# Converting the weights at a later due time, and loading w_out a second time with its columns on the partitions

## The chip, the cores and the metric

The kernel runs on one core of a Trainium2 chip. The metric is the time of one execution on the device in microseconds (us). TensorE (PE) does matmuls and transposes, VectorE (DVE), ScalarE (ACT) and GpSimd (POOL) work elementwise, and SyncE (SP) issues most of the DMAs. Each engine runs its own instructions in order; semaphores tie them together.

## The reference

There are 4 x 576 = 2304 tokens with 512 features, and three parts run one after the other.

1. Attention with 8 heads of 64 features. Half of the heads see the last 32 positions, the other half every 32nd position. Its output x is 2304 x 512.
2. A gated layer: `x = ((x @ w_a) * (x @ w_b)) @ w_out`, with w_a and w_b 512 x 1536 and w_out 1536 x 512.
3. A layer of 8 experts: `logits = x @ w_gate` (512 x 8). A greedy assignment in the order of all logits gives each expert 288 tokens, and each token passes `relu(x @ w1[e]) @ w2[e]` of its expert.

w_a, w_b and w_out arrive as float64, the other tensors as float32.

## The kernel before

**Numbers.** [...] A float64 piece (128 partitions x 512 numbers, 512 KB) is loaded as pairs of 32-bit words into a tile `r`, and `from_f64` (L444) turns it into float32 with two ACT passes (on the low words, and the magnitude of the high words) and four DVE passes (a shift and mask, a merge, an addition, and a compare-and-multiply that writes the float32 piece `w_f`; the first three write the scratch tile `cc`). `Load` (L464) does this for a pair of pieces: `start` issues the loads, `finish` converts, `store` writes the float32 result back to DRAM (`wab_dram`, `wo_dram`), from where later uses reload it. Each large matmul is done as three matmuls on high and low parts (`mm3`, L434): `split` makes `wh` on POOL and `wl` on DVE out of a weight tile.

**Stages.** x is built in blocks of 256 tokens. Hidden features come in 12 chunks f of 128. `gated(s)` (L833) computes `ab`, the products of one chunk with w_a and w_b for some blocks, and multiplies them into `G`. Stages 0 to 6 run over these blocks and chunks: 0: blocks 0, 1, f 0-2; 1: blocks 2, 3, f 0-2; 2: blocks 0-3, f 3-6; 3: blocks 0, 1, f 7-11; 4: blocks 2, 3, f 7-11; 5: blocks 4, 5, all f; 6: blocks 6-8, all f. Attention of batch 0 runs ahead of stage 0, batch 1 within stage 0, batch 2 within stage 4, batch 3 within stage 5. Stage 1 needs batch 1. A chunk's first use takes the freshly converted `w_f`; every later use reloads it from `wab_dram` into a tile `wab` of the pool `raws`, which has three buffers.

**The gate.** The logits don't wait for x: `gate_weights(js)` (L746) forms W = w_out @ w_gate for six groups j of 256 rows, and `logits` multiplies G by W. For each j it loads and converts w_out's rows (two loads through `raws`), stores them for the third part of the kernel, transposes the eight 128 x 128 squares on PE against the identity (tile `tp`), copies them from PSUM to `woT` with ACT, multiplies with w_gate (`pw`, eight matmuls), copies (`wT`), and does four small matmuls (`pw` again) that end in the table `Wp`. Groups 0, 1 run in stage 3, groups 2, 3 in stage 4, groups 4, 5 in stage 5.

**Order.** The program writes no engine order by hand. Each operation is recorded with a due time, and `flush` (L234) simulates the engines and gives each the ready operation that is due first; that order is then fixed. All records have line 163 in the profile, so the rows below go by tile names. `weave` (L382) sets the due times: a generator yields (cost, gap), costs of the running matmuls move the time t on, and the next step of a chain is due after its gap. Chains that a stage brings along (attention, the gate) are due at t less 2000 ns in most stages. One background chain, `convert(range(12))` (L789), converts w_a and w_b chunk by chunk at its own pace (a step each 500 ns, ten steps a chunk, 1000 ns between chunks); its steps are due at t + 4000. `convert` also issues the loads of the next chunk and the store. A chunk that isn't yet converted when a stage wants it is converted on the spot, at the stage's due time (`split_w`, L816). SP takes a DMA at most 40 us ahead of its due time, and the stores of w_a and w_b are held back until 52 us + 3 us per chunk of simulated time.

**Room.** The pool `big` has 18 buffers for `G` (kept from its first product on), `w_f`, `cc`, `woT`, `wT`, and the w_a, w_b tiles `r`. Twelve hold `G` of blocks 0-3 by stage 4, and six more hold that of blocks 4, 5 from the ninth chunk of stage 5 on.

In the first 70 us of simulated time, idle PE time is filled with throw-away matmuls (tile `warm`, L904).

Of the kernel before, what the change touches and what calls it, by code (L numbers as in the profile page):

```python
# [8 lines left out]
F32 = mybir.dt.float32  # L9
# [5 lines left out]
AF = mybir.ActivationFunctionType  # L15
# [344 lines left out]
def tile_attention_moe_moe(  # L360
# [4 lines left out]
    vs: bass.AP,  # L365
    w_ab: bass.AP,
    w_out: bass.AP,
    w_gate: bass.AP,
    w1: bass.AP,
    w2: bass.AP,  # L370
# [3 lines left out]
    nc = plan = Plan(tc)  # L374
# [4 lines left out]
    def at(t):  # L379
        plan.prio = t  # L380

    def weave(bulk, chains, spacing=0.0, lead=0.0):  # L382

        t = clock["t"]
        live = [[c, t] for c in chains]
        running = bulk is not None
        while running or live:  # L390
            nxt = min(live + back, key=lambda c: c[1]) if live + back else None
            if nxt is not None and (nxt[1] <= t or not running):
                t = max(t, nxt[1])
                at(t + 4000 if nxt in back else t - lead)
                try:
                    cost, gap = next(nxt[0])
                    t += cost
                    nxt[1] = t + (gap if nxt in back else max(gap, spacing))
                except StopIteration:
                    (back if nxt in back else live).remove(nxt)  # L400
            else:
                at(t)
                try:
                    t += next(bulk)[0]
                except StopIteration:
                    running = False
        clock["t"] = t
        at(t)

    back = []  # L410
# [11 lines left out]
    raws = ctx.enter_context(tc.tile_pool(name="raws", bufs=3))  # L422
    big = ctx.enter_context(tc.tile_pool(name="big", bufs=18))
# [77 lines left out]
    ident = consts.tile([128, 128], F32)  # L501
# [7 lines left out]
    for h in range(2):  # L509
        s = slice(64 * h, 64 * h + 64)  # L510
# [21 lines left out]
    def ps_tp(name):  # L532
        return psA.tile([128, 512], F32, name=name, tag="tp", bufs=2)
# [212 lines left out]
    def gate_weights(js):  # L746
        for j in js:
            ld = Load([w_out[256 * j + 128 * s:256 * j + 128 * s + 128].rearrange("p (u d) -> p u d", u=1)
                       for s in range(2)], wo_dram[j], raws)
            ld.start()  # L750
            yield 0, 5000
            for _ in ld.finish():
                yield 0, 300
            yield 0, 3000
            ld.store()
            r = ld.dst.rearrange("p (s d) -> p s d", s=2)
            woT = big.tile([128, 4, 256], F32, name="woT", tag="big")
            for s in range(2):
                p = ps_tp("tp")
                for kc in range(4):  # L760
                    nc.tensor.transpose(p[:, kc * 128:(kc + 1) * 128], r[:, s, kc * 128:(kc + 1) * 128], ident)
                nc.scalar.activation(woT[:, :, 128 * s:128 * s + 128], p.rearrange("p (k f) -> p k f", k=4), AF.Copy)
                yield 440, 0 if s == 0 else 1000
            pw = ps_tp("pw")
            for kc in range(4):
                nc.tensor.matmul(pw[32 * kc:32 * kc + 32, :256], wg[:, kc, :], woT[:, kc, :], start=True, stop=True)
            wT = big.tile([128, 256], F32, name="wT", tag="big")
            nc.scalar.activation(wT, pw[:, :256], AF.Copy)
            yield 500, 900
            pw = ps_tp("pw")  # L770
            for s in range(2):
                nc.tensor.matmul(pw[:, 8 * s:8 * s + 8], wT[:, 128 * s:128 * s + 128], lsel, start=True, stop=True)
            V.tensor_copy(Wp[:, 2 * j:2 * j + 2, :8], pw[:, :16].rearrange("p (s e) -> p s e", s=2))
            yield 430, 0
# [131 lines left out]
    def begun(r):  # L906
# [5 lines left out]
    plan.floor = 0.0  # L912

    weave(None, [attention(0, (0,)), later(0, attention(0, (1,))), later(6000, attention(0, (2,))),
                 later(8000, attention(0, (3,)))])
    split_w(0)
    plan.slack = SLACK
    weave(gated(0), [later(0, attention(1, (0,))), later(2000, attention(1, (1,))), later(6000, attention(1, (2,))), later(8000, attention(1, (3,)))], 0, 2000)
    weave(gated(1), [])
    weave(gated(2), [])  # L920
    weave(gated(3), [gate_weights((0, 1))], 100, 2000)
    weave(gated(4), [attention(2, (0, 2)), later(2000, attention(2, (1, 3))), gate_weights((2, 3))], 500, 2000)
    weave(gated(5), [attention(3), gate_weights((4, 5))], 0, 2000)
    plan.flush()
    apool_cm.__exit__(None, None, None)
# [401 lines left out]
    with ahead(40000):  # L1327
        for g in range(3):
            if g % 2 == 0:
                t = big.tile([128, 2, 512], F32, name="xg", tag="big")  # L1330
# [28 lines left out]
    def ps_po(d):  # L1359
        return ps_mm("po") if d == 3 else ps_acc("po")  # L1360
# [76 lines left out]
    with ahead(40000):  # L1437
        xs, q = [], []
        for kc in range(4):
            p = ps_tp("tpi")  # L1440
            for g in range(3):
                nc.tensor.transpose(p[:, 96 * g:96 * g + 96], XG[0][g][:, 128 * kc:128 * kc + 128], ident[:96, :96])
            t = cpool.tile([128, CAP], F32, name=f"oT{kc}", bufs=1)
# [3 lines left out]
        for kc in range(4):  # L1447
            p = ps_po(kc)
# [5 lines left out]
    for e in range(E):  # L1454
# [29 lines left out]
        for d in range(4):  # L1484
            t = cpool.tile([128, CAP], F32, name=f"oT{d}", bufs=1)
# [14 lines left out]
def _laid_out(q, k, v, moe_w_a, moe_w_b, moe_w_out, moe2_w_gate, moe2_w1, moe2_w2):  # L1500

    import numpy as np

    qk = np.zeros((16, 128, 2, 608), q.dtype)
    vl = np.zeros((8, 128, 2, 9, 64), v.dtype)
    vs = np.zeros((8, 128, 6, 2, 64), v.dtype)
    for n in range(16):
        b, hp = n // 4, (0, 2, 1, 3)[n % 4]
        i = 2 * b + n % 4 // 2
        for t, x in enumerate((q, k)):  # L1510
            y = x[b, 2 * hp:2 * hp + 2].transpose(0, 2, 1).reshape(128, S)
            o = 32 * t if hp < 2 else 0
            if hp >= 2:
                y = y.reshape(128, 18, 32).transpose(0, 2, 1).reshape(128, S)
            qk[n, :, t, o:o + S] = y
        y = v[b, 2 * hp:2 * hp + 2]
        if hp < 2:
            for c in range(9):
                a = max(0, 64 * c - 32)
                vl[i, 96 - (64 * c + 64 - a):96, :, c] = y[:, a:64 * c + 64].transpose(1, 0, 2)  # L1520
        else:
            y = y.reshape(2, 18, 32, 64)
            for odd in range(2):
                for r in range(3):
                    p, nr = 64 * odd + 18 * r, (4 if r == 2 else 5) if odd else 6
                    o = 18 * odd + r
                    vs[i, p:p + 18, :nr] = y[:, :, o:o + 3 * nr - 2:3].transpose(1, 2, 0, 3)
    w_ab = np.stack([w.reshape(4, 128, 12, 128) for w in (moe_w_a, moe_w_b)])
    return {
        "qk": qk.reshape(16, 128, 1216), "vl": vl.reshape(8, 128, 1152), "vs": vs.reshape(8, 128, 768),  # L1530
        "w_ab": w_ab.transpose(3, 2, 0, 1, 4).reshape(12, 128, 1024), "w_out": moe_w_out, "w_gate": moe2_w_gate,
        "w1": moe2_w1.reshape(E, 4, 128, 4, 256).transpose(0, 3, 2, 1, 4).reshape(E, 4, 128, 1024),
        "w2": moe2_w2.reshape(E, 4, 2, 128, DM).transpose(0, 1, 3, 2, 4).reshape(E, 4, 128, 1024)}

# [24 lines left out]
```

## Time and profile before

| | |
|---|---|
| median of 3 runs | 852.51 us (849.06 to 853.31) |
| the profiled execution | 849.75 us, span 848.0 us |
| PE busy | 825.1 us, 97% of the span, 6402 matmuls |
| DVE busy | 492.5 us, 58% |
| ACT busy | 311.8 us, 37% |
| POOL busy | 161.2 us, 19% |
| mean granted TensorE clock | 0.99 of 2.4 GHz |

The span runs from the first to the last instruction; the profiled execution has 1.75 us outside it. Matmuls are pipelined: a matmul's duration reaches over the start of the next ones, so what a matmul costs PE is read from the distance of starts, not from its duration. In the rows that list idle time, the words behind the arrow name what ended it.

### The profile page before, as it was taken

What the parts mean: (1) busy time and instruction counts of PE and PEld (TensorE: products, weight loads), DVE (VectorE), ACT (ScalarE), POOL (GpSimd) and SP (SyncE); (2) the same over time, 40 slices, a digit from 0 to 9 for tenths busy, and PEclk for the clock granted to TensorE, in tenths of its full rate; (3) what the DMA queues carried; (4) which work ended last, traced back from release to release, by engine and by line L of the source; (5) the groups of instructions that cost most, each with busy time, mean ns of one, the idle gap of its engine ahead of it and who ended that gap; (6) DMA issues with size and microseconds to landing.
All of it is one profiled execution on the core that took longest, in us unless ns stands there. A gap on an engine that the chain in (4) does not pass through costs nothing.

```text
span 848.0 us, 16546 instructions
## 1 busy us (share of the span) xinstructions
PE 825.1 (97%) x6402; PEld 698.8 (82%) x6402; DVE 492.5 (58%) x1448; ACT 311.8 (37%) x841; POOL 161.2 (19%) x219
## 2 busy tenths in 40 slices
PE   9898999999999999999999999999999999999995
PEld 7776888877787878888767777778799999999995
DVE  5999985357655431223477777766265655665541
ACT  6985531356455311111323232222233432443230
POOL 2101221110111130101000000000253425443311
PEclk9899999999999999999999999999999999999998
DMA  9779752145552211121232212100275655654501
GB/s 351 282 247 413 266 199 99 51 147 190 174 177 95 75 51 50 51 75 53 79 106 76 75 50 76 50 26 26 69 215 182 187 163 196 221 185 155 176 21 37
DMA packets 33487, 114.83 MB, mean 135 GB/s; under 512 B 4608, under 2 KB 4608, under 8 KB 33408
## 3 DMA queue, kind: packets, MB, share of 16 engines
q1 hardware_dynamic: 30336, 104.36, 35.9%
q0 software_dynamic: 3072, 9.41, 3.6%
q8 instruction: 50, 0.82, 0.4%
q14 instruction: 29, 0.24, 0.1%
HBM read 94.91 MB, written 18.87 MB: 134 GB/s over the span
## 4 chain that ended last, share of the span: by engine, by line
PE 82%; DVE 7%; DMA 3%; ACT 3%; issue 2%; POOL 2%; POOLq 0%; ACTq 0%; DVEq 0%; SPq 0%
PE ab L163 33%; PE px L163 18%; PE po L163 11%; PE ph L163 9%; PE pc L163 3%; DVE cc L163 2%; PE S L163 2%; PE pl L163 1%; DVE w12l L163 1%; PE O L163 1%; PE PT L163 1%; DVE t L163 1%; PE tpo L163 1%; POOL out_dram L163 1%; DVE xl L163 1%
## 5 line engine op out<-in xcount | busy, mean ns | idle before, releaser
L163 PE MATMUL ab<-xh,wh 128*128 128x512 f32 (+1 forms) x488 | 183.2, 376 | 1.1 <-DVE nm L163 0.8
L163 PE MATMUL ab<-xl,wh 128*128 128x512 f32 (+1 forms) x488 | 179.5, 368 | 1.7 <-DVE xl L163 1.7
L163 PE MATMUL ab<-xh,wl 128*128 128x512 f32 (+1 forms) x488 | 179.1, 367 | 0.6 <-DVE wl L163 0.6
L163 PEld LDWEIGHTS ab<-xh,wh 128*128 128x128 f32 x488 | 92.3, 189 | 21.2 <-issue 4.9
L163 DVE TENSOR_TENSOR G<-a_sb,ab 128x256 f32<-128x256 f32 x108 | 41.2, 415 | 117.9 <-PE ab L163 114.8
L163 PEld LDWEIGHTS ab<-xl,wh 128*128 128x128 f32 x488 | 92.5, 190 | 16.1 <-DVE xl L163 2.1
L163 PEld LDWEIGHTS ab<-xh,wl 128*128 128x128 f32 x488 | 92.5, 190 | 16.0 <-DVE wl L163 0.9
L163 DVE TENSOR_TENSOR w12l<-w,w12h 128x1024 fp32r<-128x1024 f32 x64 | 78.5, 1234 | 40.5 <-PE po L163 31.7
L163 PE MATMUL px<-woh,gh 128*128 128x512 f32 x216 | 87.2, 404 | 0.3 <-ACT gh L163 0.3
L163 PE MATMUL px<-wol,gh 128*128 128x512 f32 x216 | 87.2, 404 | 0.0
L163 ACT ACTIVATE a_sb<-ab 128x512 f32<-128x512 f32 (+1 forms) x61 | 33.3, 546 | 138.4 <-PE ab L163 119.9
L163 POOL TENSOR_SCALAR wh<-wab 128x1024 fp32r<-128x1024 f32 x32 | 35.9, 1122 | 234.5 <-PE ab L163 210.0
L163 PE MATMUL po<-hh,w12h 128*128 128x288 f32 x256 | 76.7, 300 | 0.0
L163 ACT ACTIVATE gh<-G 128x512 fp32r<-128x512 f32 x54 | 34.1, 632 | 115.8 <-PE px L163 101.5
L163 PE MATMUL ph<-xeh,w12h 128*128 128x288 f32 x256 | 75.1, 304 | 1.4 <-DVE hl L163 0.7
L163 PE MATMUL po<-hh,w12l 128*128 128x288 f32 x256 | 75.7, 296 | 0.0
L163 PE MATMUL po<-hl,w12h 128*128 128x288 f32 x256 | 75.6, 296 | 0.0
L163 PE MATMUL ph<-xel,w12h 128*128 128x288 f32 x256 | 75.2, 296 | 0.3
L163 PE MATMUL ph<-xeh,w12l 128*128 128x288 f32 x256 | 74.7, 297 | 0.0
L163 ACT ACTIVATE w12h<-w 128x1024 fp32r<-128x1024 f32 x36 | 38.2, 1060 | 60.5 <-PE po L163 42.7
L163 PEld LDWEIGHTS ph<-xel,w12h 128*128 128x128 f32 x256 | 48.7, 190 | 1.7 <-DVE xel L163 1.6
L163 PEld LDWEIGHTS ph<-xeh,w12h 128*128 128x128 f32 x256 | 47.3, 188 | 2.8 <-DVE hl L163 2.3
(369 smaller groups left out, 1539.6 us busy)
## 6 DMA issues: line engine op xcount, KB each, us to landing
w<-in_w_dram SPq DMA_DIRECT2D x64, 512.0 KB, 3.6
wab<-wab_dram SPq DMA_DIRECT2D x32, 512.0 KB, 3.3
r<-in_w_ab_dram SPq DMA_DIRECT2D x24, 512.0 KB, 8.4
qkT<-in_qk_dram SPq DMA_DIRECT2D x16, 608.0 KB, 5.9
wab_dram<-w_f SPq DMA_DIRECT2D x12, 512.0 KB, 7.8
r<-in_w_out_dram SPq DMA_DIRECT2D x12, 512.0 KB, 3.5
x_dram<-xr SPq DMA_DIRECT2D x17, 256.0 KB, 2.1
vt<-in_vl_dram SPq DMA_DIRECT2D x7, 576.0 KB, 7.2
```

The lines of the kernel that those rows point to most:

```text
L163: op.call = lambda: getattr(engine, method)(*args, **kwargs)
```

## The change

The array `w_outT` holds the same float64 numbers as `w_out`, laid out by the host so that a group's 512 columns stand on the partitions (4 x 128) and its 256 rows follow one another. `gate_weights` still loads, converts and stores w_out's rows as before, and then loads and converts the same group from `w_outT`; the converted tile takes the place of `woT`. The transposes and the ACT copies out of PSUM are gone. The gap between the end of a conversion and what follows is 1500 ns where it was 3000. In `weave`, the background chain's steps are due at t + 12000 where it was t + 4000.

```diff
@@ weave
-                at(t + 4000 if nxt in back else t - lead)
+                at(t + 12000 if nxt in back else t - lead)
@@ gate_weights
             for _ in ld.finish():
                 yield 0, 300
-            yield 0, 3000
+            yield 0, 1500
             ld.store()
-            r = ld.dst.rearrange("p (s d) -> p s d", s=2)
-            woT = big.tile([128, 4, 256], F32, name="woT", tag="big")
-            for s in range(2):
-                p = ps_tp("tp")
-                for kc in range(4):
-                    nc.tensor.transpose(p[:, kc * 128:(kc + 1) * 128], r[:, s, kc * 128:(kc + 1) * 128], ident)
-                nc.scalar.activation(woT[:, :, 128 * s:128 * s + 128], p.rearrange("p (k f) -> p k f", k=4), AF.Copy)
-                yield 440, 0 if s == 0 else 1000
+            lt = Load([w_outT[j][:, 512 * t:512 * t + 512].rearrange("p (k f) -> p k f", k=2) for t in range(2)], None, raws)
+            lt.start()
+            yield 0, 5000
+            for _ in lt.finish():
+                yield 0, 300
+            yield 0, 1500
+            woT = lt.dst.rearrange("p (k f) -> p k f", k=4)
             pw = ps_tp("pw")
@@ _laid_out
+        "w_outT": moe_w_out.reshape(6, 256, 4, 128).transpose(0, 3, 2, 1).reshape(6, 128, 1024), "w_gate": moe2_w_gate,
```

## Rows read from the trace of the kernel before

**Rows 1.** Chain that ended last, 0 to 80 us: its shares by line.
```profile
by line: DVE cc L163 20.0%; DVE t L163 9.1%; issue 8.0%; DVE w_f L163 7.6%; PE warm L904 7.4%; ACT P L163 6.5%; DVE xl L163 6.3%; DVE wl L163 4.3%; PE ab L163 4.2%; DVE P L163 3.6%; PE S L163 3.5%; ACT Ps L163 3.2%; PE PT L163 2.4%; DVE Ps 
```

**Rows 2.** Windows, early: length, then busy PE, PEld, DVE, ACT, POOL; clock, DMA.
```profile
40.00:60.00 20.00, 17.93 (x221) 15.14 (x221) 20.00 (x102) 16.64 (x82) 1.61 (x4) 1.00 0.60 197
60.00:80.00 20.00, 17.22 (x193) 13.18 (x192) 19.70 (x49) 13.81 (x40) 2.82 (x5) 1.00 1.03 410
100.00:120.00 20.00, 20.00 (x90) 16.57 (x89) 19.44 (x37) 8.39 (x14) 7.50 (x2) 1.00 0.67 233
```

**Rows 3.** PE in order of time, 26 to 78 us: start, duration, operation [idle before].
```profile
26.96 0.80 PE L163 MATMUL ab<-xh,wl 128*128 128x256 f32 x2 [0.60 <-DVE wl L163]
...
77.49 0.50 PE L163 MATMUL ab<-xl,wh 128*128 128x512 f32 x1 [1.70 <-DVE xl L163]
```

**Rows 4.** Windows of 14 to 77.5 us, instructions on `cc` alone: their sum.
```profile
sum 63.50, DVE 32.84 ACT 9.91; mean DVE 8.21 ACT 2.48
```

**Rows 5.** The same windows, instructions on `w_f` alone: their sum.
```profile
sum 63.50, PE 0.00 PEld 0.00 DVE 13.13 POOL 3.37; mean PE 0.00 PEld 0.00 DVE 3.28 POOL 0.84
```

**Rows 6.** All engines in order of time: the first reload of stage 1.
```profile
69.47 1.05 POOL L163 TENSOR_SCALAR wh<-wab 128x1024 fp32r<-128x1024 f32 x1 [16.09 <-DMA wab<-wab_dram]
...
71.58 1.21 DVE L163 TENSOR_TENSOR wl<-wab,wh 128x1024 fp32r<-128x1024 f32 x1
```

**Rows 7.** Tile `tp`: duration in ns min/median/max, first and last start in us.
```profile
L163 PE MATMUL tp<-ident,w_f x48: 270/273/330, 151.5 to 259.6; 128*128 128x128 f32 x48
L163 ACT ACTIVATE woT<-tp x12: 570/592/599, 152.2 to 260.2; 128x512 f32<-128x512 f32 x12
```

**Rows 8.** PE in order of time: transposes and the next PE operation behind them.
```profile
151.54 1.03 PE L163 MATMUL tp<-ident,w_f 128*128 128x128 f32 x8
152.33 0.48 PE L163 MATMUL ab<-xh,wh 128*128 128x512 f32 x1
...
183.72 0.66 PE L163 MATMUL tp<-ident,w_f 128*128 128x128 f32 x4
184.21 0.49 PE L163 MATMUL PT<-ident,P 128*96 128x128 f32 x3
...
258.79 1.03 PE L163 MATMUL tp<-ident,w_f 128*128 128x128 f32 x8
259.76 0.88 PE L163 MATMUL S<-qkT 64*64 64x96 f32 x16
```

**Rows 9.** Tiles `r`, `cc` and `w_f`: the passes of all 36 conversions, columns as in Rows 7.
```profile
L163 ACT ACTIVATE r<-r x36: 654/677/708, 14.2 to 236.5; 128x512 int32<-128x512 uint32 x36
L163 DVE TENSOR_SCALAR cc<-r x36: 409/419/1276, 15.2 to 240.4; 128x512 int32<-128x512 int32 x36
L163 DVE SCALAR_TENSOR_TENSOR cc<-r,cc x36: 617/683/726, 15.7 to 240.8; 128x512 int32<-128x512 int32 x36
L163 DVE CUSTOM_DVE_ANT_0 cc<-r,cc x36: 671/683/1533, 16.6 to 241.6; 128x1024 uint16<-128x1024 uint16 x36
L163 DVE SCALAR_TENSOR_TENSOR w_f<-cc x36: 629/683/1271, 17.9 to 244.4; 128x512 f32<-128x512 f32 x36
```

**Rows 10.** Windows of stages 3 to 5, columns as in Rows 2.
```profile
135.00:151.50 16.50, 16.50 (x74) 13.65 (x73) 10.24 (x18) 1.79 (x3) 3.32 (x4) 1.00 0.25 96
187.30:197.30 10.00, 8.27 (x122) 6.24 (x121) 5.49 (x31) 7.52 (x33) 0.17 (x1) 0.83 0.73 250
213.00:280.00 67.00, 66.63 (x593) 53.19 (x593) 36.32 (x135) 31.92 (x117) 10.81 (x15) 1.00 0.42 135
```

**Rows 11.** SP and DVE in order of time: a gate piece, and a reloaded chunk.
```profile
176.91 0.33 SPq L163 DMA_DIRECT2D r<-in_w_out_dram  x1
...
184.46 0.69 DVE L163 CUSTOM_DVE_ANT_0 cc<-r,cc 128x1024 uint16<-128x1024 uint16 x1
...
234.83 0.33 SPq L163 DMA_DIRECT2D wab<-wab_dram  x1
...
248.69 1.22 DVE L163 TENSOR_TENSOR wl<-wab,wh 128x1024 fp32r<-128x1024 f32 x1
```

More of the change, by code (lines that the diff above doesn't have):

```diff
@@ L367, in tile_attention_moe_moe @@
     w_out: bass.AP,
+    w_outT: bass.AP,
     w_gate: bass.AP,
@@ L1530, in _laid_out @@
         "qk": qk.reshape(16, 128, 1216), "vl": vl.reshape(8, 128, 1152), "vs": vs.reshape(8, 128, 768),
-        "w_ab": w_ab.transpose(3, 2, 0, 1, 4).reshape(12, 128, 1024), "w_out": moe_w_out, "w_gate": moe2_w_gate,
+        "w_ab": w_ab.transpose(3, 2, 0, 1, 4).reshape(12, 128, 1024), "w_out": moe_w_out,
+        "w_outT": moe_w_out.reshape(6, 256, 4, 128).transpose(0, 3, 2, 1).reshape(6, 128, 1024), "w_gate": moe2_w_gate,
         "w1": moe2_w1.reshape(E, 4, 128, 4, 256).transpose(0, 3, 2, 1, 4).reshape(E, 4, 128, 1024),
```

## The prediction

> **What bounds the kernel now.** I read the windows by stage first, because the page's 97% for PE hides two regimes. From 78 us on PE has work nearly all the time; stage 5 has 66.63 of 67 us busy [rows 10]. There, PE work that goes is time that goes. Before 78 us it is otherwise: from 40 to 60 us PE is busy 17.93 of 20 us and DVE all 20, from 60 to 80 us PE 17.22 and DVE 19.70 [rows 2]. The reader is to see that DVE is the full engine and PE the one that waits, 4.85 us in these 40. The chain of waits for the first 80 us agrees: the largest single share is the conversion, 20.0% on `cc` and 7.6% on `w_f`, more than the softmax of attention, 9.1% on `t` [rows 1]. The end of this regime is a wait of PE: stage 1 has begun and stops for 1.70 us until 77.49 us for an `xl`, the last piece of attention of batch 1 [rows 3]. From there on PE runs through, so a start of stage 1 that is earlier by some time ends the kernel earlier by the same, if nothing new waits.
>
> One hole lies in the second regime. From 187.3 to 197.3 us, where stage 4's matmuls are short and attention of batch 2 ends, PE is busy 8.27 of 10 us at a granted clock of 0.83 [rows 10]. 1.73 us are idle, and the mean clock of 0.83 means that the lower level (1.2 in place of 2.4 GHz) took another 0.17 x 10 = 1.7 us, behind the thin work there.
>
> **The transposes.** 48 transposes go, in nine runs: three of 8 and six of 4. A transpose lasts 273 ns [rows 7], but eight of them start within 1.03 us. The cost on PE is the distance from the first of a run to the next other operation: 152.33 - 151.54 = 0.79 us for the first run, 184.21 - 183.72 = 0.49 for one of four, 259.76 - 258.79 = 0.97 for the last [rows 8]. The nine distances sum to 2.72 (the eights) + 2.87 (the fours) = 5.6 us. One of the fours, 0.5 us, lies in the hole, where PE waits anyway. So 5.1 us come off the end. The bounds are 0, if PE waited at each place for something else, and 48 x 0.273 = 13.1 us, if a transpose cost its duration. The distance is the nearest row to what is asked, and I take it.
>
> The Trainium skill (TensorE: Matmul & The Clock Gate, Part 4: PE-mode transpose) gives about 275 ns for a 128 x 128 transpose in one kernel's context and says that access latency is most of it. The duration in this trace agrees [rows 7]; the distances of the starts do not let it be taken as the cost. By the page's figure the saving would be 13.2 us, an estimate.
>
> Twelve ACT copies of 0.592 us go with them, 7.1 us [rows 7], on an engine that is busy 1.79 of 16.5 us there [rows 10].
>
> **The second load and conversion.** Per group two loads of 512 KB and two conversions, so 12 of each. A conversion is four DVE passes, 0.419 + 3 x 0.683 = 2.47 us by their durations, and two ACT passes of about 0.68 us [rows 9]. That is 48 passes or 29.6 us more on DVE, and 24 passes or 16.2 us more on ACT (9.1 net of the copies). What hides them: in the first part of stage 3 DVE is free for 16.5 - 10.24 = 6.3 us, in stage 5 for 67 - 36.3 = 30.7 us, while PE is full [rows 10]; four conversions, 9.9 us, belong to each of stages 3, 4 and 5. Their consumer, the eight `pw` matmuls, is off the path: `Wp` is wanted in stage 6. If the cover is gone, an attention step of batch 2 or 3 waits behind one pass, 0.68 us each time; the place where that shows is the hole, since there the tail of batch 2 sets PE's pace. I charge nothing, with bounds of 0 and 3.4 us, the size of the hole again. DMA takes 6.3 MB more where its share is 0.25 to 0.73 [rows 10].
>
> On SP twelve issues of about 0.33 us are added [rows 11], and they wait there for a buffer of `raws`; what is queued behind them are the reloads `wab` and the loads of attention. That is the slow rival below.
>
> By its yields a group's chain was due over 5000 + 3000 + 3000 + 440 + 1440 + 1400 + 430 = 14.7 us and is now over 20.8 us. It ends nearer to the chunk of stage 5 from which G fills all 18 buffers of `big`, but PE doesn't wait for a group until then.
>
> **The later due time.** Nothing is added; per chunk two loads, four ACT passes, eight DVE passes and a store move behind what is due in the next 8 us. On DVE and ACT these are softmax and output steps of attention, on SP the loads of q, k and v. A chunk takes 1000 + 10 x 500 = 6.0 us of due time, so 1.3 chunks, 2.7 conversions, 6.6 us of DVE work, move behind the end of batch 1. There is enough to move: by 77.5 us DVE has spent 32.84 + 13.13 = 46.0 us on conversions [rows 4, 5], with four passes a piece about 18 pieces, while stages 0 and 1 want only six. The work isn't lost: DVE stays full to 120 us (19.44 of 20 from 100 to 120 [rows 2]) and has room after that.
>
> How much of it PE gets is bounded twice. It can't win more than the 4.85 us that it waits. And stage 1 needs the reloaded chunk 0: its `wh` waited for the DMA and ended at 69.47 + 1.05 = 70.5 us, its `wl` ended at 72.8 [rows 6]; with DVE free at once `wl` would end at 71.7. So stage 1 can begin 1.1 us earlier and lose its stop of 1.70 us [rows 3]: 2.8 us. The lower bound is a loss: PE has already waited 0.60 us for the first `wl` at 26.96 us [rows 3], and chunk 0's conversion is moved too; up to 2 us, an estimate, since what PE does there is a few 256-column matmuls ahead of attention's last head. I take 2.0 us of gain, nearer to the upper end, because the row that ends the regime is attention and not the weights.
>
> **Sum.** 5.1 + 2.0 = 7.1 us off the profiled execution: 849.75 (848.0 of span and 1.75 around it) becomes 842.6. The median of the runs stands 2.76 us above the profiled one, so the forecast against it is 852.5 - 7.1 = 845.4 us.
>
> **Rivals.**
>
> - The due time changes nothing: stage 1 is held by the reload, which waits for a store that is held back to 52 us; for it speaks that POOL waited 16.09 us for that DMA [rows 6], against it the stop on `xl`. 852.5 - 5.1 = 847.4.
> - The hole grows: four added conversions in stage 4 press on the tail of batch 2, and PE loses another 3.4 us of idle time and clock. For it: ACT is busy 7.52 of 10 us there [rows 10]. Against: the transposes are gone from the same stretch. 848.8.
> - The hole closes, because the new order puts stage 5's first matmuls into it: 842.0. For it: `ab` of stage 5 is ready soon after; against: nothing in the change aims at it.
> - Slower: the three buffers of `raws`. A gate piece holds its buffer from its load to its last read, 184.46 + 0.69 - 176.91 = 8.2 us, and `wab` reloads take buffers in turn behind it. Four added pairs fall in stages 4 and 5. Against it: a reload is issued far ahead, the shortest lead that I found being 248.69 - 234.83 = 13.9 us [rows 11]. One pair in front is hidden; it decides from two pairs, 16.4 us, on; three in front of one chunk cost 24.6 - 13.9 = 10.7 us, which gives 856, and twice that 867.
> - A transpose costs its duration: 852.5 - 13.1 - 2.0 = 837.4. The starts within 1.03 us [rows 8] speak against it.
>
> **How the numbers follow.** Forecast 0.38, no effect of the due time 0.20, hole grows 0.17, hole closes 0.12, `raws` 0.11, full duration 0.02. About 0.5%, 4.3 us, is what a measurement can tell from no change: below 848.2 is faster, above 856.8 slower. Faster: 0.34 + 0.13 + 0.05 + 0.12 + 0.02 = 0.66, taken down to 0.62, because an order that is made anew can open waits that no row names; slower 0.10, most of it from `raws`; the same 0.28. The range is 839 to 854: the lower end leaves out the full duration and holds a hole that closes together with the whole 2.8 us, the upper end leaves out `raws`.
>
> **What would show it.** Right: no `tp`; PE's stop before stage 1 gone or under 0.5 us, and the first dense stretch beginning near 75 us; 48 instead of 36 of each conversion pass, at the same durations; PE full from stage 1 on. Wrong: PE waiting on `wl` or `wh` in stages 4 and 5 with SP waiting for `raws` before it; a wait of `pw` on `w_f`; a second low-clock stretch; attention of batch 1 ending as late as now.

## The result and the profile after

The changed kernel takes 861.32 us (median of 5 runs, 858.51 to 862.94) beside 852.51 us of the kernel before (849.06 to 853.45): a ratio of 1.0117, 95% interval 1.0094 to 1.014. It is slower by 8.8 us where 7.1 us less was forecast, and outside the range. The profiled execution takes 860.41 us with a span of 858.7.

To see where the time went, take the start of the first `ab` matmul of each stage on PE in both traces; what lies between two of these marks has the same `ab` matmuls in it.

| first `ab` matmul | before | after | difference |
|---|---|---|---|
| stage 2 | 91.02 | 88.38 | -2.64 |
| stage 3 | 134.53 | 131.90 | -2.63 |
| fifth and last chunk of stage 3 | 158.52 | 153.66 | -4.86 |
| stage 4 | 166.49 | 167.47 | +0.98 |
| stage 5 | 216.92 | 216.29 | -0.63 |
| stage 6 | 303.50 | 313.77 | +10.27 |

By stage 2 the kernel is 2.6 us ahead. By the fifth chunk of stage 3 it is 4.9 us ahead. Only 0.79 us of this further 2.2 are the first group's eight transposes [rows 8]; most of the rest is that the group's `pw` matmuls have not been done yet and lie behind this mark now. From there to stage 6, where most of the second loads and their conversions lie, it loses 15.1 us (12.9 from the start of stage 3). After that little happens (10.7 us at the end of the profiled spans).

The windows of the changed kernel, in the columns of [rows 2], for the stretches of [rows 2, 10], and 150 to 310 us:

```profile
40.00:60.00 20.00, 18.61 (x211) 14.91 (x206) 20.00 (x89) 19.33 (x83) 2.75 (x8) 1.00 0.72 223
60.00:80.00 20.00, 17.45 (x146) 13.22 (x146) 20.00 (x46) 9.90 (x27) 4.43 (x3) 1.00 1.03 412
135.00:151.50 16.50, 16.50 (x75) 13.65 (x74) 16.16 (x24) 3.47 (x6) 3.63 (x3) 1.00 0.24 96
187.30:197.30 10.00, 8.93 (x133) 7.52 (x133) 5.75 (x21) 5.56 (x20) 0.00 (x0) 0.83 0.69 239
213.00:280.00 67.00, 59.05 (x506) 46.33 (x507) 53.70 (x153) 34.56 (x117) 9.60 (x14) 1.00 0.60 199
150.00:310.00 160.00, 144.88 (x1203) 113.40 (x1202) 114.22 (x361) 79.12 (x278) 22.05 (x30) 0.97 0.53 173
```

Stage 5 is the surprise: PE was busy 66.63 of these 67 us [rows 10] and is now busy 59.05. Over 150 to 310 us PE stands idle for 15.1 us; before it was 2.1:

```profile
150.00:310.00 160.00, 157.90 (x1327) 125.74 (x1326) 85.04 (x310) 72.14 (x267) 28.21 (x54) 0.99 0.38 127
```

DVE is now busy 114.22 of 160 us and ACT 79.12: neither is full. The list of PE's waits in the changed kernel in the same 160 us (us in total, times, longest) says who is late:

```profile
PE O L163 <- ACT PT L163: 6.0, 4, 2.3
PE pw L163 <- ACT wT L163: 5.9, 2, 4.3
PE pw L163 <- DVE w_f L163: 1.4, 1, 1.4
PE O L163 <- ACT PTs L163: 1.3, 2, 0.8
```

Three of the four, 13.2 us, are ACT copies of 0.3 to 0.6 us out of PSUM, on an engine that is half idle. What ACT waited for, in the same stretch:

```profile
ACT r L163 <- DMA r<-in_w_outT_dram: 20.5, 8, 5.3
ACT r L163 <- DMA r<-in_w_out_dram: 7.3, 4, 2.3
```

and in the kernel before:

```profile
ACT r L163 <- DMA r<-in_w_out_dram: 4.6, 3, 2.7
```

So ACT now stands for 27.8 us at the first pass of a conversion, whose words aren't there yet, and as it runs in order, what is queued behind that pass stands too. (DVE's first pass waits for the words as well, but less: from 130 to 315 us DVE stood 5.7 us for these loads, 3.9 before.) Two of the places in order of time (start, duration, operation, idle before), first ACT:

```profile
160.50 0.68 ACT L163 ACTIVATE r<-r 128x512 int32<-128x512 uint32 x1 [2.56 <-DMA r<-in_w_outT_dram]
161.08 0.65 ACT L163 ACTIVATE cc<-r 128x512 f32<-128x512 f32 x1
163.92 0.67 ACT L163 ACTIVATE r<-r 128x512 int32<-128x512 uint32 x1 [2.19 <-DMA r<-in_w_outT_dram]
164.50 0.36 ACT L163 ACTIVATE wT<-pw 128x256 f32<-128x256 f32 x1
...
279.02 0.68 ACT L163 ACTIVATE r<-r 128x512 int32<-128x512 uint32 x1 [5.34 <-DMA r<-in_w_outT_dram]
279.60 0.73 ACT L163 ACTIVATE PT<-PT 96x128 f32<-96x128 f32 x2
```

and PE at these places:

```profile
164.91 0.61 PE L163 MATMUL pw<-lsel,wT 128*128 128x8 f32 x4 [4.28 <-ACT wT L163]
...
187.93 0.69 PE L163 MATMUL O<-PT,vt 96*64 96x64 f32 x16 [2.31 <-ACT PT L163]
...
221.20 0.62 PE L163 MATMUL pw<-w_f,wg 128*32 128x256 f32 x4 [1.37 <-DVE w_f L163]
...
279.90 1.16 PE L163 MATMUL O<-PT,vt 96*64 96x64 f32 x20 [2.08 <-ACT PT L163]
```

`wT` at 164.50 is a copy of 0.36 us that belongs to the group whose conversion is over; PE has had nothing to do since 160.63 and waits for it, and it stands behind the passes of the next load, the last of which waits 2.19 us for its words. `PT` at 279.60 is attention's, behind a wait of 5.34. The chain of waits from 150 to 300 us (start, us, what) shows the whole loop at the first place:

```profile
157.23 1.14 DVE wl L163
158.37 0.02 issue
158.39 5.45 DMA r<-in_w_outT_dram
...
163.92 0.04 ACT r L163
163.97 0.53 issue
164.50 0.37 ACT wT L163
164.87 0.04 issue
164.91 0.61 PE pw L163 x4
```

The load didn't start before DVE had read a reloaded chunk (`wl`) and with that given back its buffer of `raws`; it then took 5.45 us. The load behind the wait of 2.08 us starts after a `wl` too (at 274.74), the one behind the wait of 2.31 us after a pass on `cc` (at 180.53). The loads of `w_outT` make up 20.6% of this chain.

Three of these waits are paid for a second time. The granted clock falls to 0.50, the lower of its two levels (1.2 GHz), soon after each has ended, though PE is then busy without a break. The profile's page shows nothing of it, because its slices are 21 us wide; windows of half a microsecond do:

```profile
165.00:165.50 0.50, 0.50 (x6) 0.48 (x6) 0.00 (x0) 0.41 (x1) 0.00 (x0) 1.00 0.98 385
165.50:166.00 0.50, 0.50 (x12) 0.50 (x12) 0.44 (x2) 0.00 (x0) 0.00 (x0) 0.62 0.69 279
166.00:166.50 0.50, 0.50 (x11) 0.40 (x8) 0.50 (x4) 0.00 (x0) 0.00 (x0) 0.50 0.03 8
...
190.00:190.50 0.50, 0.50 (x2) 0.37 (x2) 0.50 (x2) 0.00 (x0) 0.00 (x0) 0.50 0.98 396
...
282.00:282.50 0.50, 0.50 (x2) 0.40 (x2) 0.20 (x1) 0.33 (x1) 0.00 (x0) 0.50 1.04 147
```

From stage 3's first `ab` to stage 6's, what the clock granted less than 1.00 adds up to 5.1 us of PE time, 1.7 us for each of the three; before there was one, 1.7 us, in the hole of stage 4.

### The profile page after: what moved, and what is told of

It reads as the page before. It is cut to its first block, busy times and chain, and to the rows that moved or that the text cites. A ratio compares the mean times of both kernels' runs of the same rounds, so it can differ in the third digit from the quotient of the medians.

```text
span 858.7 us, 16529 instructions
## 1 busy us (share of the span) xinstructions
PE 822.8 (96%) x6344; PEld 693.4 (81%) x6344; DVE 523.6 (61%) x1496; ACT 319.1 (37%) x853; POOL 159.6 (19%) x219
## 4 chain that ended last, share of the span: by engine, by line
PE 62%; DVE 11%; DMA 11%; issue 8%; ACT 5%; POOL 3%; POOLq 0%; ACTq 0%; DVEq 0%; SPq 0%
PE ab L163 18%; PE px L163 17%; PE po L163 11%; PE ph L163 7%; DMA r<-in_w_outT_dram 4%; PE pc L163 3%; DVE cc L163 3%; DMA w<-in_w_dram 2%; DVE wl L163 2%; POOL wh L163 2%; DMA r<-in_w_out_dram 1%; DVE w12l L163 1%; PE pl L163 1%; ACT P L163 1%; DVE w_f L163 1%
## 5 line engine op out<-in xcount | busy, mean ns | idle before, releaser
L163 POOL TENSOR_SCALAR wh<-wab 128x1024 fp32r<-128x1024 f32 x32 | 37.9, 1184 | 243.6 <-PE ab L163 223.2
L163 ACT ACTIVATE r<-r 128x512 int32<-128x512 uint32 x48 | 32.6, 680 | 45.5 <-DMA r<-in_w_outT_dram 22.4
```

Of the source, the lines that this page charges most:

```text
L163: op.call = lambda: getattr(engine, method)(*args, **kwargs)
```

## The experiments

**The theory** (queue): the planner reckons that a load's words are there some 3.45 us after its issue, and puts the conversion's first pass into ACT's and DVE's order by that. The second load starts late, on a freed buffer, and lands later than reckoned: the median was 5.2 us for `w_outT` and 4.2 us for `w_out` (3.5 before). The pass blocks ACT's queue, and copies that PE needs stand behind it. **Rivals**: the added passes themselves cost the time (work); the due time or the traffic does; any new order falls well or badly (luck). Each run is compared with runs of the kernel before that were taken beside it; these had a median of 849.98 us beside e1 to e4, 850.58 beside e5 to e8, and 850.49 beside e9 to e12.

**e1, the due time alone** (kernel before).

```diff
-                at(t + 4000 if nxt in back else t - lead)
+                at(t + 12000 if nxt in back else t - lead)
```

> The kernel before with the later due time alone (t + 12000), transposes kept. Three theories for the 8.8 us that the change lost. Queue theory: ACT and DVE hold a pass of the second conversion whose load lands late, and copies that PE needs (PT, wT) stand behind it. Work theory: the added 48 DVE and 24 ACT passes slow attention of batches 2 and 3, whoever waits for a load. Due theory: the conversion of w_a and w_b, moved by 8 us, comes late. Queue and work theory expect what the trace of the changed kernel shows by the start of stage 2, 2.6 us earlier, and nothing lost behind it: 849 to 851 us. The due theory expects 858 us or more.

Measured 844.94 us, ratio 0.9917 (0.9887 to 0.9946), less than the 849 to 851 us expected. Stages 2 to 4 begin 1.94 us earlier, as forecast; stage 5 begins 3.87 us earlier, because the hole of stage 4 [rows 10] now runs at the full clock:

```profile
187.30:197.30 10.00, 9.27 (x151) 7.82 (x152) 8.17 (x54) 8.27 (x44) 1.05 (x1) 1.00 0.79 263
```

So the due time isn't where the change loses. It gains by itself, 5.0 us by the medians where I gave it 2.0; in the trace the part beyond the forecast is the hole.

**e2, the second load and conversion without the due time** (changed kernel).

```diff
-                at(t + 12000 if nxt in back else t - lead)
+                at(t + 4000 if nxt in back else t - lead)
```

> The changed kernel with the old due time (t + 4000): second load and conversion, no transposes. Queue and work theory: the loss is all here, and the 2.6 us of the later due time are missing: 863 to 865 us, with PE waiting 10 us or more for ACT's PT and wT between 150 and 300 us. Due theory: 848 to 852 us.

Measured 859.62 us, ratio 1.0103 (1.007 to 1.0137), a little less than the 863 to 865 us expected. This part alone makes the kernel slower. From 130 to 315 us ACT waits 21.0 us for the w_out loads, PE 8.3 us for ACT.

**e3, no transposes and no second load** (kernel before; the gate's matmuls read w_out's rows untransposed).

```diff
-            for s in range(2):
...
-                    nc.tensor.transpose(p[:, kc * 128:(kc + 1) * 128], r[:, s, kc * 128:(kc + 1) * 128], ident)
...
+            woT = ld.dst.rearrange("p (k f) -> p k f", k=4)
```

> The kernel before (t + 4000) without the transposes and without a second load: the gate's matmuls read w_out's converted rows as they lie, so the logits, and with them the assignment, differ; the amount of work behind is the same. What the removal alone is worth. By the distances of the starts 5.1 us: 846 to 849 us. By the durations of the transposes 13 us: 839 to 841 us. If PE waits at those places anyway: 852 us.

Measured 847.63 us, ratio 0.9956 (0.9934 to 0.9978), and stage 6 begins 4.65 us earlier. The ratio stands for 1.9 to 5.6 us. That fits the price by the distances of starts, 5.1 us, and not the 13.1 us by durations. The Trainium skill (TensorE: Matmul & The Clock Gate, Part 4: PE-mode transpose) gives about 275 ns for one, and the trace has that as a duration [rows 7]; as a cost on a full PE the measurement decides, 4.65 / 48 = 0.10 us.

**e4, the plan told that these loads land later** (changed kernel; the step between a load's data and its reader counted with 4000 ns in place of 1050, for the gate's loads alone; the kernel's work and transfers stay the same).

```diff
-            return 1050.0
+            return a.hop
...
+                plan.landing = 4000.0 if self.pool is raws else 1050.0
```

> The changed kernel with the same operations, but the order is made with loads of w_out and w_outT counted as landing 2.95 us later (4000 in place of 1050 ns behind the transfer), so that their conversion passes take a later place in the queues of ACT and DVE. Queue theory: most of the 15 us that PE stands idle between 150 and 300 us goes, 846 to 853 us. Work theory: the same passes on the same engines, 859 us or more. If buffers of raws are what delays the loads more than the landing, part of it stays: 853 to 858 us.

Measured 848.38 us, ratio 0.9973 (0.9954 to 0.9991): some 13 us better than the changed kernel, with the same instructions in another order. ACT's waits from 150 to 310 us:

```profile
ACT r L164 <- DMA r<-in_w_outT_dram: 2.6, 2, 2.2
ACT r L164 <- DMA r<-in_w_out_dram: 0.8, 1, 0.8
```

The loads land no sooner (medians 4.9 and 4.1 us), and DVE does as much in the stretch (114.40 us busy, 114.22 in the changed kernel). With e8 and e10 below this separates the wait from the work: the same passes run in 844 to 848 us, and the work theory falls.

**e5, the second conversion without a second load** (changed kernel; it converts the rows' words once more, so W comes out of the untransposed numbers).

```diff
-            lt.start()
+            lt.r, lt.begun = ld.r, True
```

> The changed kernel with its second conversion, but without the second load: the 48 DVE and 24 ACT passes run over the words of w_out that the first conversion has read, in the same buffers (the gate's matmuls so get rows that aren't transposed, and the assignment differs). Queue theory: no pass of the second conversion can wait for a load, so the ACT waits for in_w_outT of 20.5 us are gone and the time is 839 to 848 us. Work theory: the same passes, 857 us or more.

Measured 846.92 us, ratio 0.9955 (0.9931 to 0.9979), within the queue theory's interval. But the premise didn't come: from 130 to 315 us ACT stood 23.2 us for the first load, `w_out`, alone, and PE still waits 5.0 us for ACT. So the run shows that the added passes don't cost the time by themselves; it doesn't show what the wait for the second load costs.

**e6, the second load without its conversion** (changed kernel; a short POOL copy reads each piece, and W comes out of the untransposed numbers).

```diff
-            for _ in lt.finish():
...
+            for r in lt.r:
+                nc.gpsimd.tensor_copy(sink2, r.bitcast(I32)[:, :1])
```

> The changed kernel with its second load and without the second conversion: each loaded piece is read by one short POOL copy of one column, which frees its buffer (again the gate gets rows that aren't transposed). Queue theory: nothing on ACT or DVE stands behind these loads, 838 to 846 us. If the 6.3 MB more, or the buffers of raws, cost by themselves (reloads of weights late), 850 us or more, with PE waiting for wl or wh in stages 4 and 5.

Measured 841.08 us, ratio 0.9906 (0.9874 to 0.9938). All of the change's traffic and all of its turns in `raws` are in it, and its median is the lowest of all runs here. POOL waited 36.2 us for these loads from 130 to 315 us, and PE never waited for POOL there. So traffic and buffers show no cost of their own, and the same loads cost PE nothing when POOL waits for them. One wait for ACT is left, 3.4 us for a `PTs` that stands behind a first pass of `w_out`.

**e7, the due time alone with the later landing** (e1 with e4's edit).

```diff
+                plan.landing = 4000.0 if self.pool is raws else 1050.0
```

> The later due time and the later landing in the order's making (4000 for 1050 ns), with the transposes and without a second load. Queue theory: the first load of w_out makes ACT wait 4.7 us in the kernel with the due time alone, so a little is to be had: 842 to 846 us. If the first load's waits are hidden: 845 us as with the due time alone.

Measured 845.67 us, ratio 0.9941 (0.9918 to 0.9963), not told apart from e1. Without the second load the later landing gains nothing that shows.

**e8, the later landing at 2500 ns** (changed kernel, e4's edit with a smaller step).

```diff
+                plan.landing = 2500.0 if self.pool is raws else 1050.0
```

> As the changed kernel with loads counted as landing later, but by half as much (2500 in place of 4000; the changed kernel has 1050). The measured median landing is 5.2 us against some 3.4 that the order reckons with, so 1.5 us more should reach the median but not the late ones. Queue theory: between 848 and 861 us, 850 to 856. If it is a matter of one order against another by luck and not of the landing, no such step in between: anything from 848 to 862 us.

Measured 843.99 us, ratio 0.9919 (0.9896 to 0.9943). The smaller step does better than 4000, against my expectation. The windows of three stretches, to set beside those of the changed kernel, and ACT's waits from 150 to 310 us:

```profile
187.30:197.30 10.00, 10.00 (x78) 8.15 (x75) 7.24 (x42) 7.50 (x41) 2.38 (x2) 1.00 0.61 208
213.00:280.00 67.00, 66.36 (x528) 51.61 (x527) 53.49 (x166) 37.27 (x130) 10.19 (x12) 1.00 0.56 188
150.00:310.00 160.00, 157.28 (x1328) 123.20 (x1327) 114.95 (x364) 80.81 (x281) 27.21 (x54) 1.00 0.52 176
```

```profile
ACT r L164 <- DMA r<-in_w_outT_dram: 5.0, 4, 2.0
...
ACT r L164 <- DMA r<-in_w_out_dram: 3.1, 1, 3.1
```

All the conversions are there (DVE 53.49 of 67 us in stage 5, as in the changed kernel), and PE is full beside them. Stage 6 begins 7.31 us earlier than before. This is the changed kernel in another order, and it beats both the changed kernel and the one before. It does not beat e1 (844.94): the due time brings the gain, and nothing here shows that the second load is worth more than the transposes.

**e9, another order without the cure** (changed kernel).

```diff
-                at(t + 12000 if nxt in back else t - lead)
+                at(t + 8000 if nxt in back else t - lead)
```

> The changed kernel with the background chain due at t + 8000 where the change has 12000, the plan's landing left as it is: another order, without the cure. Queue theory (a conversion pass that stands in ACT's order ahead of copies and waits for its load): ACT still waits 15 us or more for the words of the second load between 150 and 310 us, PE waits 2 us or more at a time for PT or wT copies, 856 to 863 us. Luck theory (any new order may fall well, and the landing cured by chance): no tie between ACT's wait for loads and the time; anything from 845 to 860 us.

Measured 851.23 us, ratio 1.0 (0.9978 to 1.0022): a miss for the time. From 150 to 310 us:

```profile
ACT r L163 <- DMA r<-in_w_outT_dram: 13.8, 6, 5.2
ACT r L163 <- DMA r<-in_w_out_dram: 9.1, 5, 2.5
```

ACT stands nearly as long, 22.9 us, but PE idles 7.0 us (152.98 of 160 busy) in place of 15.1. So the wait at the head of ACT's queue isn't the price. The price is what stands behind it, and that is up to the order. In that much the luck theory is right: an order that only looks different gave back 10 us, where the later landing gives 13 to 17.

**e10, the later landing at 1800 ns** (changed kernel).

```diff
+                plan.landing = 1800.0 if self.pool is raws else 1050.0
```

> The changed kernel, with the plan told that the loads of the gate's pieces land 0.75 us later (a step of 1800 ns where it counts 1050), half of the step that gave 844.0 us. Queue theory: ACT's wait for the second load lies between the 20.5 us of the changed kernel and the 5.0 us at 2500; time between too, 846 to 856 us. Luck theory: no order by the size of the step.

Measured 845.73 us, ratio 0.9941 (0.9921 to 0.9961), just below the interval I gave. ACT's wait for the second load, 9.9 us, lies between those of 1050 and 2500 (20.5 and 5.0). The wait falls with each step of the landing (20.5, 9.9, 5.0, and 2.6 us at 4000); the time doesn't (861.32, 845.73, 843.99, 848.38).

**e11, the fault put into the kernel before**: its loads of w_out counted as landing 2.05 us earlier. No work is added, none taken away.

```diff
+                plan.landing = -1000.0 if self.pool is raws else 1050.0
```

> The kernel before, with the plan told that its w_out loads land 2.05 us earlier than it counts (-1000 ns where it counts 1050): the fault put in without any of the change's work. Queue theory: the passes on r stand in ACT's order before their words are there, ACT's wait for w_out loads grows from 4.6 us to over 10 us, PE waits for copies behind them, 853 to 858 us. Work theory (the added conversions themselves cost the time): as before, 849 to 852 us.

Measured 862.69 us, ratio 1.014 (1.0119 to 1.0162): as slow as the change, and slower than I expected. ACT, and PE behind it:

```profile
189.61 0.67 ACT L164 ACTIVATE r<-r 128x512 int32<-128x512 uint32 x1 [2.64 <-DMA r<-in_w_out_dram]
...
216.82 0.68 ACT L164 ACTIVATE r<-r 128x512 int32<-128x512 uint32 x1 [3.04 <-DMA r<-in_w_out_dram]
```

```profile
194.47 0.67 PE L164 MATMUL PT<-ident,Ps 128*128 128x128 f32 x3 [3.09 <-DVE Ps L164]
...
217.81 0.45 PE L164 MATMUL O<-PT,vt 96*64 96x64 f32 x8 [2.25 <-ACT PT L164]
```

The wait of 3.09 us goes back to ACT too: behind the pass at 189.61 stands the copy `xh`, behind that an `xl` in DVE's order, and behind that the `Ps` for which PE waits. Of the 11.38 us by which stage 6 begins later, 2.88 are there by stage 2 and 8.5 come between stages 4 and 6. The latter is PE's idle time, 9.0 us from stage 3 to 6 where it was 2.1, and a second fall of the clock, 3.4 us lost where it was 1.7. The 2.88 can't be put down to the new order, which differs from the old one on no engine before 83 us: they are there by then, and 1.7 of them are a fall of the clock at 78.66 us.

**e12, the control** (kernel before, its w_out loads counted as landing 1.45 us later).

```diff
+                plan.landing = 2500.0 if self.pool is raws else 1050.0
```

> Control: the kernel before, with the plan told that its w_out loads land 1.45 us later (2500 where it counts 1050). Queue theory: the kernel before has 4.6 us of ACT waits for these loads and hardly a wait of PE behind them, so at most 2 us to gain: 848 to 851 us. If the later landing helped for another reason than the second load, it would gain here what it gained on the changed kernel, some 15 us.

Measured 849.62 us, ratio 0.9984 (0.9967 to 1.0001). The same edit that took 17 us off the changed kernel does nothing measurable here, though it takes ACT's waits for these loads from 9.0 to 1.5 us.

**Side by side.** The first two columns are waits from 130 to 315 us: ACT's for loads of `w_out` and `w_outT`, PE's for ACT. The next three split the time between the first `ab` of stage 3 and that of stage 6: PE idle; lost to the lower clock (each window's length times what its granted clock is below 1.00); and the rest, PE busy at the full clock. Their sum is that time.

| | ACT for loads | PE for ACT | idle | clock | rest | sum | median |
|---|---|---|---|---|---|---|---|
| before | 9.0 | 0.2 | 2.1 | 1.7 | 165.2 | 169.0 | 849.98 to 852.51 |
| after | 27.8 | 13.2 | 15.1 | 5.1 | 161.7 | 181.9 | 861.32 |
| e1 | 14.4 | 0.2 | 1.8 | 0.0 | 165.2 | 167.0 | 844.94 |
| e2 | 21.0 | 8.3 | 10.1 | 1.7 | 162.1 | 173.9 | 859.62 |
| e3 | 7.4 | 1.7 | 3.0 | 1.7 | 159.3 | 164.0 | 847.63 |
| e4 (4000) | 3.4 | 0.7 | 5.1 | 0.0 | 162.0 | 167.2 | 848.38 |
| e5 | 23.2 | 5.0 | 5.9 | 3.4 | 160.0 | 169.3 | 846.92 |
| e6 | 8.6 | 3.4 | 3.8 | 3.4 | 159.2 | 166.4 | 841.08 |
| e7 (4000) | 1.7 | 1.8 | 2.2 | 1.7 | 164.7 | 168.7 | 845.67 |
| e8 (2500) | 11.6 | 1.1 | 2.7 | 0.0 | 161.4 | 164.1 | 843.99 |
| e9 | 36.3 | 5.5 | 7.0 | 5.1 | 160.5 | 172.6 | 851.23 |
| e10 (1800) | 16.2 | 2.2 | 5.3 | 0.0 | 161.7 | 167.0 | 845.73 |
| e11 | 19.1 | 5.4 | 9.0 | 3.4 | 165.0 | 177.5 | 862.69 |
| e12 | 1.5 | 0.8 | 1.6 | 0.0 | 164.9 | 166.5 | 849.62 |

The first column goes with the loss only loosely (e1 has 14.4 and no loss, e9 the most and half the loss); idle time and clock make the difference between the orders. The rest says whether the transposes are there: 165 with them, 159 to 160 without them in e3, e5 and e6.

**Open.** With both the second load and its conversion the rest is 160.5 to 162.1, in all orders, 0.5 to 2.9 us more than in e3, e5 and e6, though the same matmuls run in it; so 3.5 us of the transposes' 5.6 come off in the changed kernel. About half of the other 2 is in the eight `pw` matmuls: by the distances of starts a run of eight takes 0.57 us, and a run of four 0.56. In e8 and e10 two of the six groups have their eight in two runs of four, and the `pw` on `w_f` take 4.50 us in all; before and in e3, with all six in runs of eight, they take 3.35 and 3.42. What takes the other half stays open. Why 4000 is worse than 2500 isn't settled: PE waits there 2.1 us for `xl` of DVE where e8 has 0.8, but what holds DVE was not tested. The split explains one profiled execution of each kernel, and that can lie some us off the median (e3: 844.85 for 847.63, e2: 856.66 for 859.62, e12: 847.05 for 849.62, e6: 844.75 for 841.08); for the size of an effect the medians and their ratios decide. The first 90 us alone can differ that much: up to 81 us all engines have the same order in all kernels with the same due time, and stage 2 yet begins between 89.63 and 93.90 us in the five traces with t + 4000 and between 88.38 and 90.92 in the eight with t + 12000. That the landing alone, and not a new order as such, cures the change is not shown: e9 and the steps of 1800, 2500 and 4000 are four orders, and each has its own places where PE waits. More buffers in `raws` were not tried.

## Why the prediction was wrong, step by step

- **The due time, -2.0 us.** Right in size: stage 2 began 2.64 us earlier, stage 2 of e1 1.94, and over all traces it begins at a mean of 89.0 us with the later due time and 91.5 without. Not by the two bounds, though. Stage 1 began 4.31 us earlier (68.22 for 72.53) where I allowed 1.1 by the reloaded chunk; that chunk came earlier as well (its `wh` ended at 66.99 for 70.5). The stop on `xl`, 1.70 us [rows 3], is 0.30 now, but stage 1 then took 20.16 us for 18.49, with short waits for `wl` and `wh` (0.67, 0.72, 0.59 us). That these errors nearly cancel is luck.
- **The transposes, -5.1 us.** Right: 4.65 by stage 6 in e3; the distance of the starts was the price, and not the duration. In the change some 1.1 us of it are paid back, because two of the groups have their `pw` in two runs.
- **The second load and conversion, "I charge nothing, with bounds of 0 and 3.4 us".** This is the step that failed. Their work was counted rightly (DVE 523.6 us busy after 492.5, +31.1 for 29.6 reckoned; ACT +7.3 for 9.1) and there was room for it. But between the first `ab` of stage 3 and of stage 6 PE's idle time grew by 13.0 us and what the clock took by 3.4, 16.4 us where I charged nothing. I looked for cover in busy shares and let an attention step wait "behind one pass, 0.68 us each time". A pass doesn't hold its queue for its 0.68 us; it holds it until its load has landed. And "Their consumer, the eight `pw` matmuls, is off the path" held only for `Wp`, which is wanted late. PE runs in order as well, so a `pw` whose input is late stops the attention and `ab` matmuls behind it: 7.3 us of the waits (5.9 for `wT`, 1.4 for `w_f`) are on `pw`, another 7.3 on attention. In the kernel before the trace already showed such waits on ACT, one of 4.35 us that ended at 131.58 and three of up to 2.7 from 150 us on, with PE hardly touched by them (0.2 us of waits for ACT). I didn't read ACT's own list of waits, and the change doubles the loads of which these waits are made.
- **"Slower: the three buffers of `raws`"**, 856 or 867 at a chance of 0.11. The right resource and the wrong victim. I had the reloads late; the list of PE's waits from 150 to 310 us has none for `wl` or `wh`. Late was the second load itself, which at two of the three long waits started only when `wl` had read a reload, and its passes hold ACT. The rival's sign, PE waiting on `wl` or `wh` in stages 4 and 5, didn't come; that of `pw` waiting on `w_f` did, once, 1.37 us.
- **"The hole closes", 842.0.** Its fall of the clock is gone in e1, e4, e8, e10 and e12, by the order alone: in e12 nothing but the reckoned landing was changed. In the changed kernel that stretch has a clock of 0.83 again, but the fall lies at 189.51 us behind the wait for `PT`, where it was at 193.54. In e2, e3, e5, e6, e7 and e9 falls lie elsewhere between 163 and 273 us.
- **The sum.** In an order that hardly stalls (e8) stage 6 begins 7.31 us earlier, for 7.1 forecast. That is partly luck: the hole is closed there, which the sum left open, and the rest falls by 3.8 us and not by 5.1. But it is the size that was forecast, and the term that the sum lacked is the order.

## What to carry to other kernels

When an instruction that waits for a DMA is added to an engine that runs in order, its price here wasn't its duration but the wait at its head, and who pays is whoever is queued behind it. So ask of each added load when it can start (whose buffer it takes), when it lands, and which short copy for the full engine stands behind its first reader. Where a plan fixes the order, its landing time is a tuning value: 0.75 us more of it was worth 15.6 us here (861.32 to 845.73, against 852.51 and 850.49 of the kernel before), and 2.05 us less cost the kernel before 1.4%. More isn't better (4000 lost to 2500), and a shifted due time (e9) gave 10 us too. Before crediting an edit, run its parts alone, and an order that only looks different.

## What the hardware showed that I had not expected

- The same kind of transfer, 512 KB, lands later when there are more of them: a median of 3.5 us before, 4.2 (`w_out`) and 5.2 us (`w_outT`) after, the DMA share from 150 to 310 us going from 0.38 to 0.53; in e8, at 0.52, 3.9 and 4.4.
- A wait of PE can be paid for a second time, and its length doesn't tell whether it is. Behind the waits of 4.28, 2.31 and 2.08 us, which ended at 164.91, 187.93 and 279.90 us, the clock fell 0.7 to 1.8 us later and cost 1.7 us each, with PE busy throughout. Behind the waits of 1.37 and 1.64 us that ended at 221.20 and 227.77 it stayed at 1.00. In e3 a wait of 1.29 us that ended at 209.54 was followed by a fall at 210.49; in e2 a longer one was not, and from 276.9 to 282 us the clock stayed at 1.00:

```profile
276.92 1.17 PE L163 MATMUL O<-PT,vt 96*64 96x64 f32 x20 [2.03 <-ACT PT L163]
```

- Four `pw` matmuls in a row cost PE as much as eight: 0.56 us and 0.57 us by the distance of the starts.
